# Attention scores of two heads in one four-bank PSUM tile, subtractions moved from POOL to DVE, more bias units ahead, and one account that shares work between DVE and ACT

## The chip, the cores and the metric

The kernel runs on one core of a Trainium2 chip. A core has five engines with a queue each: TensorE (PE, with PEld for the loading of its weights), VectorE (DVE), ScalarE (ACT), GpSimd (POOL) and SyncE (SP), which here issues the DMAs. Each engine takes its instructions in the order of its queue. The metric is the time of one execution on the device in microseconds (us); lower is better. All tensors are fp32 in DRAM.

## The reference

Attention with a learned relative bias (B = 2 batches, H = 8 heads, S = 576 positions, D = 64), then two gated feed-forward layers over 1152 tokens of 512 features with 1536 hidden features:

```python
scores = scale * (q @ k.T)                                   # per batch and head
x = log1p(abs(i - j)) / log1p(max(i, 1))                     # per pair of positions
bias = relu(x[..., None] @ w1 + b1) @ w2                     # 32 hidden features, 8 heads
attn = softmax(scores + bias); y = attn @ v                  # 2, 8, 576, 64
x = y.transpose(0, 2, 1, 3).reshape(1152, 512)
x = ((x @ w_a) * (x @ w_b)) @ w_out                          # first layer
x = (silu(x @ w_gate) * (x @ w_val)) @ w_out                 # second layer
```

## The kernel before, in words

**Products.** A matrix product in fp32 is made of three products of a rounded high part and a remainder: high by high, high by low, low by high. So q has the parts `qa` and `qb`, k has `ka` and `kb`, the attention's output `xh` and `xl`, the feed-forward weights `wh` and `wl`. A high part is a copy that rounds (a cast), a low part the source minus the high part (a subtraction).

**Bias units.** The bias of 16 rows for all eight heads is a unit; there are 36 (`Bias.make`, L119). A unit has four instructions `hidden` (L109 on DVE or L111 on ACT, tiles `hd`), four to eight matmuls (L133) into a one-bank PSUM tile `tp`, two to four instructions `scaled` (L115 on DVE or L117 on ACT) into `bt`, and one DMA that writes `bt` to `bias_d` in DRAM (L146). Whether DVE or ACT takes a `hidden` or a `scaled` is decided by `Bias.take` with an account of these instructions alone. Twelve units are emitted first (L303), then two in each of the first twelve steps (L309).

**Steps of the attention.** There are 20 steps, each for a pair of heads `p`, a group `g` of query tiles and one tile `t` of 128 rows (L307). Heads `2p` and `2p+1` lie on partitions 0 to 63 and 64 to 127 of q and k. A step loads its bias rows from `bias_d` (L325; for t = 4, the last 64 rows of both batches, into two padded tiles `pad`, L329), then calls `scores` (L231), once for each batch, or once for t = 4. A call of t < 4 has twelve matmuls (L238) of 288 columns: two halves of the columns, three products, two heads `j`; the two heads use different halves of the rows of the array. There are 32 such calls, and four of t = 4 with 24 matmuls of 320 columns. The results lie in two PSUM tiles `ps` of two banks, one for each head, from a pool of two (L216, L233). For each head one DVE instruction (L241) adds the bias, writes `es` to SBUF and finds the row maximum `nm`; ACT makes the exponential (L245). Then PE transposes `es` in chunks of 128 columns into `tp` (L263), and `keep` (L250) copies each three chunks to `ee`, on ACT (L253) ten times of sixteen, else on DVE (L255).

**The end of a pair and group** (`finish`, L266): row sums `rs` (L272 to L275, DVE), `rw` (L277, ACT), its transposes (L282), `rc` (L287, ACT), the products with v into `pu` (L291), `t` (L293, DVE), then the high part `xh` on ACT (L300) and the low part `xl` on POOL (L301). The q and k of the next pair are loaded by SP at the first step of a pair and split by `Heads.split`: cast on DVE (L157), subtraction on POOL (L158).

**The feed-forward stage** (`moe`, L372) starts after the attention. It has 2592 matmuls (L389) of 384 columns; DVE and ACT decode its weights (L201 to L207), and POOL subtracts (L208).

**What sets the order.** The program text is not the order of the queues. A scheduler simulates the engines, and puts each instruction into its engine's queue at the time at which it expects it to be ready; `issue_after` holds an instruction back behind another. Buffers are handed on as tiles come free.

Of the kernel before, what the change touches and what calls it, by code (L numbers as in the profile page):

```python
# [50 lines left out]
def attention_moe_moe(ctx: ExitStack, tc: tile.TileContext, qd, kd, vd, cst, lm, wm1, wm2, out):  # L51
# [10 lines left out]
    with (  # L62
        tc.tile_pool(name="prep", bufs=2) as prep,
        tc.tile_pool(name="a4", bufs=3) as a4,
    ):
        heads = Heads(tc, prep, qd, kd, vd)
        bias = ExitStack()
        bias.enter_context(tc.tile_pool(name="bc", bufs=1, side="right"))
        units = Bias(tc, bias, cst, lm, bias_d, heads)
        ends = attention(ctx, tc, a4, heads, bias, units, bias_d, xh, xl, weights, ident)  # L70
    moe(tc, xpool, xh, xl, weights, out, ends)


class Bias:
# [7 lines left out]
    def __init__(self, tc, stack, cst, lm, bias_d, heads):  # L82
        nc = self.nc = tc.nc
        self.tc, self.bias_d = tc, bias_d
# [15 lines left out]
        self.spent = {"dve": 0.0, "act": 0.0}  # L100

    def take(self, dve, act):
        eng = "dve" if self.spent["dve"] + dve <= self.spent["act"] + act else "act"
        self.spent[eng] += dve if eng == "dve" else act
        return eng == "dve"

    def hidden(self, dst, n, m):
        if self.take(DFIX + n * DMASK, AFIX + n * AELEM):
            self.nc.vector.tensor_scalar(dst, self.LW[:, :n], self.bp[:, m : m + 1], 0.0, op0=ALU.add, op1=ALU.max)  # L109
# [3 lines left out]
    def scaled(self, dst, src, n, u):  # L113
        if self.take(DFIX + n * DCOPY, AFIX + n * AELEM):
# [34 lines left out]
class Heads:  # L149


    def __init__(self, tc, pool, qd, kd, vd):
        self.nc, self.pool, self.d, self.got = tc.nc, pool, (qd, kd, vd), {}
# [57 lines left out]
def attention(ctx, tc, a4, heads, bias, units, bias_d, xh, xl, weights, ident):  # L211
    nc = tc.nc
    with (
        tc.tile_pool(name="ac", bufs=1, reuse_waits="tile") as cpool,
        tc.tile_pool(name="a2", bufs=2, reuse_waits="tile") as a2,
        tc.tile_pool(name="ps2", bufs=2, reuse_waits="tile", space=PSUM) as ps2,  # L216
# [14 lines left out]
        def scores(p, i, ops, n, es, bt):  # L231

            ps = [ps2.tile([P, 2, 512], F32, tag="big", name="ps") for j in range(2)]  # L233
            for hf in range(2):
                for m, (lt, rt) in enumerate(ops):
                    for j in range(2):
                        r = slice(64 * j, 64 * j + 64)
                        nc.tensor.matmul(ps[j][:, hf, :n], lt[r], rt[r, n * hf : n * hf + n], start=m == 0, stop=m == len(ops) - 1)  # L238
            for j in range(2):
                nm = a4.tile([P, 1], F32, tag="nm", name="nm")  # L240
                nc.vector.tensor_tensor_reduce(  # L241
                    out=es[j].rearrange("p (a j) -> p a j", a=2), in0=ps[j][:, :, :n], in1=bt[j].rearrange("p (a j) -> p a j", a=2),
                    op0=ALU.add, op1=ALU.min, scale=-0.125, scalar=3.0e38, accum_out=nm,
                )
                nc.scalar.activation(es[j], es[j], AF.Exp, bias=nm, scale=-1.0, accum_out=sums[:, 2 * p + j, i : i + 1])  # L245

        turn = [0]
# [18 lines left out]
        def finish(p, g, ee):  # L266
# [12 lines left out]
            for b in range(B):  # L279
# [7 lines left out]
                nc.scalar.copy(rc[:, :n], rb[:, :n])  # L287
# [5 lines left out]
                nc.vector.tensor_tensor(t1[:, :n], pu[:, :n], rc[:, :n], op=ALU.mult)  # L293
                s0 = place(b, g)
# [14 lines left out]
        made = (2, 2, 2, 2, 2, 2, 2, 2, 2, 2, 2, 2)  # L309
        ee = {}  # L310
        for idx, (p, g, t) in enumerate(steps):
            if idx < len(made):
# [206 lines left out]
```

## Time and profile before

| | us |
|---|---|
| median of three runs | 733.45 (731.39 to 737.64) |
| the profiled execution | 736.44 |
| its span from the first to the last instruction | 734.7 |
| PE busy in the span | 684.2 (93%) |
| DVE busy | 473.6 (64%) |
| ACT busy | 326.3 (44%) |
| POOL busy | 162.4 (22%) |

The profile is one execution; its times are in microseconds from the start of the span. Busy time of an engine counts overlapping instructions once. PEclk is the clock granted to TensorE as a share of full speed. In a timeline row, the bracket at the end is the idle time of the engine just before the instruction and what ended it. A row of the grouped view gives the count, the busy time, the mean nanoseconds of one, and the idle time ahead of the group with the releasers. The attention's score matmuls run from the first steps until about 250 us; the feed-forward stage follows.

### The profile page before, as it was taken

The numbers are of one execution on the slowest core, as the hardware profiler recorded it, in microseconds if no ns is written. First come the engines' busy times: TensorE is split into PE (matmuls) and PEld (weight loads), VectorE is DVE, ScalarE is ACT, GpSimd is POOL, SyncE is SP. The second block draws the span as 40 slices with busy tenths as digits, with TensorE's granted clock in tenths as the row PEclk, the third lists the DMA queues.
The fourth block names the chain that finished last, engine by engine and source line by source line (L and its number), as shares of the span: only waits on it lengthen the run. The fifth ranks groups of instructions, "written<-read, shape, count | busy, mean of one in ns | idle before, by whom it ended". The sixth has DMA issues, their size and how long they took to land. (4 is left out here: it accounts for less than half of the span.)

```text
span 734.7 us, 10847 instructions
## 1 busy us (share of the span) xinstructions
PE 684.2 (93%) x4112; PEld 597.1 (81%) x4112; DVE 473.6 (64%) x877; ACT 326.3 (44%) x688; POOL 162.4 (22%) x131
## 2 busy tenths in 40 slices
PE   5669699999999989999899999999989999999997
PEld 2236465656667769988899999999989999999997
DVE  7674676965677379999936993269951896232222
ACT  4636555767557456444413342245432552121110
POOL 3020051212332033332302332144410430020000
PEclk9985789999989999999999999999989999999999
DMA  3774345525566024443411440024330241000111
GB/s 108 206 237 153 113 140 178 155 66 187 164 226 181 7 87 144 144 139 118 145 58 33 137 146 29 1 72 130 118 112 1 89 153 45 1 1 1 44 43 44
DMA packets 26516, 76.35 MB, mean 104 GB/s; under 512 B 2656, under 2 KB 4320, under 8 KB 26464
## 3 DMA queue, kind: packets, MB, share of 16 engines
q1 hardware_dynamic: 26464, 75.66, 32.5%
q8 instruction: 32, 0.52, 0.3%
q14 instruction: 20, 0.16, 0.1%
HBM read 62.40 MB, written 13.25 MB: 103 GB/s over the span
## 5 line engine op out<-in xcount | busy, mean ns | idle before, releaser
L208 POOL TENSOR_TENSOR wl<-m,wh 128x512 fp32r<-128x512 f32 x72 | 99.9, 1390 | 253.8 <-ACT wh L207 223.3
L410 DVE TENSOR_TENSOR g<-p,g 128x384 f32<-128x384 f32 x72 | 39.8, 553 | 128.2 <-PE p L389 128.2
L389 PE MATMUL po<-gh,wh 128*128 128x384 f32 x288 | 98.5, 344 | 10.1 <-DVE acc L440 7.3
L389 PE MATMUL p<-xh,wh 128*128 128x384 f32 x288 | 97.2, 339 | 2.2 <-ACT g L409 2.2
L389 PE MATMUL po<-gh,wl 128*128 128x384 f32 x288 | 97.5, 339 | 0.0
L389 PE MATMUL po<-gl,wh 128*128 128x384 f32 x288 | 97.5, 339 | 0.0
L389 PE MATMUL p<-xl,wh 128*128 128x384 f32 x288 | 97.2, 338 | 0.0
L389 PE MATMUL p<-xh,wl 128*128 128x384 f32 x288 | 97.1, 337 | 0.0
L389 PE MATMUL p<-yh,wh 128*128 128x384 f32 x288 | 96.9, 337 | 0.0
L389 PE MATMUL p<-yh,wl 128*128 128x384 f32 x288 | 96.9, 337 | 0.0
L389 PE MATMUL p<-yl,wh 128*128 128x384 f32 x288 | 96.9, 336 | 0.0
L205 DVE SCALAR_TENSOR_TENSOR m<-raw,m 128x512 uint32<-128x512 uint32 x72 | 81.4, 1130 | 1.5
L412 ACT CAST gh<-g 128x384 fp32r<-128x384 f32 x72 | 36.9, 513 | 96.0 <-DVE g L410 96.0
L201 ACT ACTIVATE m<-raw 128x512 f32<-128x512 f32 x72 | 48.8, 679 | 61.1 <-POOL wl L208 60.1
L409 ACT ACTIVATE g<-p 128x384 f32<-128x384 f32 x72 | 34.9, 486 | 85.0 <-PE p L389 84.6
L245 ACT ACTIVATE es<-es,nm 128x576 f32<-128x576 f32 (+1 forms) x72 | 56.2, 782 | 27.3 <-DVE nm L241 26.4
L389 PEld LDWEIGHTS po<-gh,wh 128*128 128x128 f32 x288 | 54.7, 190 | 14.2 <-DVE acc L440 6.0
L207 ACT CAST wh<-m 128x512 fp32r<-128x512 f32 x72 | 44.2, 620 | 46.0 <-DVE m L206 42.5
L241 DVE CUSTOM_DVE_ANT_0 es<-ps,bt 128x576 f32<-128x576 f32 x64 | 46.9, 752 | 22.5 <-DMA bt<-bias_d 10.3
L263 PE MATMUL tp<-ident,es 128*128 128x128 f32 x328 | 55.0, 304 | 6.2 <-DVE bt L115 5.1
L238 PE MATMUL ps<-ka,qa 64*128 64x288 f32 (+1 forms) x160 | 52.1, 376 | 9.0 <-DVE nm L241 9.0
L206 DVE SCALAR_TENSOR_TENSOR m<-raw,m 128x512 uint32<-128x512 uint32 x72 | 58.8, 817 | 1.0
(64 smaller groups left out, 1278.2 us busy)
## 6 DMA issues: line engine op xcount, KB each, us to landing
raw<-in_wm SPq DMA_DIRECT2D x72, 512.0 KB
bias_d<-bt SPq DMA_DIRECT2D x36, 295.5 KB
bt<-bias_d SPq DMA_DIRECT2D x32, 288.0 KB
vv<-in_vd SPq DMA_DIRECT2D x8, 640.0 KB
kr<-in_kd SPq DMA_DIRECT2D x8, 576.0 KB
pad<-bias_d SPq DMA_DIRECT2D x16, 144.0 KB
out_t<-acc SPq DMA_DIRECT2D x12, 192.0 KB
raw<-in_qd SPq DMA_DIRECT2D x4, 352.0 KB
```

Source lines behind the costliest of these rows:

```text
L201: nc.scalar.activation(m, hi.bitcast(F32), AF.Abs)
L205: nc.vector.scalar_tensor_tensor(t, lo, 29, t, op0=ALU.logical_shift_right, op1=ALU.bitwise_or)
L206: nc.vector.scalar_tensor_tensor(t, hi, 0xC0000000, t, op0=ALU.bitwise_and, op1=ALU.bitwise_or)
L207: nc.scalar.copy(wh[:, i], m)
L208: nc.gpsimd.tensor_tensor(wl[:, i], m, wh[:, i].bitcast(F32), op=ALU.subtract)
L238: nc.tensor.matmul(ps[j][:, hf, :n], lt[r], rt[r, n * hf : n * hf + n], start=m == 0, stop=m == len(ops) - 1)
L241: nc.vector.tensor_tensor_reduce(out=es[j].rearrange("p (a j) -> p a j", a=2), in0=ps[j][:, :, :n], in1=bt[j].rearrange("p (a j) -> p a j" ...
L245: nc.scalar.activation(es[j], es[j], AF.Exp, bias=nm, scale=-1.0, accum_out=sums[:, 2 * p + j, i : i + 1])
L263: nc.tensor.transpose(tp[:, n], es[:, P * kc : P * kc + P], ident)
L389: nc.tensor.matmul(ps, lt, rt, start=first and n == 0, stop=last and n == len(parts) - 1)
L410: nc.vector.tensor_tensor(g, pp[1], g, op=ALU.mult)
L412: nc.scalar.copy(gh, g)
```

## The change

- `scores` writes to one PSUM tile of four banks for both heads, from a pool of one. The twelve matmuls are written in the same order.
- The low parts of q, k and of the attention's output are made on DVE instead of POOL. The low parts of the feed-forward weights, and of the output of the first layer, stay on POOL.
- The casts of q and k, `keep`, and the copy `rc` may be on DVE or ACT: one account `Share` of the work of both engines decides this, with `hidden` and `scaled`. It also counts, without choosing, the maxima and exponentials, the subtractions, `t` and `xh`. Its prices are new.
- `MADE` makes four units in each of the first two steps and two in each of the next eight.
- The calls of t = 4 are held behind the last DVE `hidden` of the twelfth unit (`lag`).

```diff
+MADE = (4, 4, 2, 2, 2, 2, 2, 2, 2, 2)
 HDS, BTS = 8, 4
-DFIX, DMASK, DCOPY = 160.0, 0.52, 1.04
-AFIX, AELEM = 280.0, 0.86
-
-SHARE = 10
+DFIX, DFAST, DSLOW = 70.0, 0.52, 1.04
+AFIX, AELEM = 190.0, 0.86
...
+class Share:
+    def __init__(self):
+        self.spent = [0.0, 0.0]
+
+    def dve(self, n, slope=DSLOW):
+        self.spent[0] += DFIX + n * slope
+
+    def act(self, n, more=0.0):
+        self.spent[1] += AFIX + n * AELEM + more
+
+    def on_dve(self, n, slope=DSLOW):
+        d, a = DFIX + n * slope, AFIX + n * AELEM
+        first = self.spent[0] + d <= self.spent[1] + a
+        self.spent[0 if first else 1] += d if first else a
+        return first
...
     def hidden(self, dst, n, m):
-        if self.take(DFIX + n * DMASK, AFIX + n * AELEM):
+        if self.share.on_dve(n, DFAST):
...
     def scaled(self, dst, src, n, u):
-        if self.take(DFIX + n * DCOPY, AFIX + n * AELEM):
+        if self.share.on_dve(n):
...
-        self.nc.vector.tensor_copy(hi[:, : n[0]], raw[:, : n[0]])
-        self.nc.gpsimd.tensor_tensor(lo[:, : n[0]], raw[:, : n[0]], hi[:, : n[0]].bitcast(F32), op=ALU.subtract)
+        w = n[0]
+        if self.share.on_dve(w, DFAST):
+            self.nc.vector.tensor_copy(hi[:, :w], raw[:, :w])
+        else:
+            self.nc.scalar.copy(hi[:, :w], raw[:, :w])
+        self.share.dve(w)
+        self.nc.vector.tensor_tensor(lo[:, :w], raw[:, :w], hi[:, :w].bitcast(F32), op=ALU.subtract)
...
-        tc.tile_pool(name="ps2", bufs=2, reuse_waits="tile", space=PSUM) as ps2,
+        tc.tile_pool(name="ps2", bufs=1, reuse_waits="tile", space=PSUM) as ps2,
...
-            ps = [ps2.tile([P, 2, 512], F32, tag="big", name="ps") for j in range(2)]
+            ps = ps2.tile([P, 2, 2, 512], F32, tag="big", name="ps")
...
-                        nc.tensor.matmul(ps[j][:, hf, :n], lt[r], rt[r, n * hf : n * hf + n], start=m == 0, stop=m == len(ops) - 1)
+                        nc.tensor.matmul(ps[:, j, hf, :n], lt[r], rt[r, n * hf : n * hf + n], start=m == 0, stop=m == len(ops) - 1)
...
+                share.dve(2 * n, 1.3)
+                share.act(2 * n, 190.0)
...
         def keep(dst, src):
-            turn[0] += 1
-            if turn[0] * SHARE % 16 < SHARE:
+            if share.on_dve(dst.free_size() if hasattr(dst, "free_size") else 384):
+                ends[1] = nc.vector.tensor_copy(dst, src)
+            else:
                 ends[0] = nc.scalar.copy(dst, src)
-            else:
-                ends[1] = nc.vector.tensor_copy(dst, src)
...
-                nc.scalar.copy(rc[:, :n], rb[:, :n])
+                if share.on_dve(n):
+                    nc.vector.tensor_copy(rc[:, :n], rb[:, :n])
+                else:
+                    nc.scalar.copy(rc[:, :n], rb[:, :n])
...
-                        nc.gpsimd.tensor_tensor(xl[c][:, p, a - CH * c : e - CH * c], src, dh.bitcast(F32), op=ALU.subtract)
+                        nc.vector.tensor_tensor(xl[c][:, p, a - CH * c : e - CH * c], src, dh.bitcast(F32), op=ALU.subtract)
...
+        lag = units.last
...
-                scores(p, 8, ops, 320, es, bt)
+                with tc.issue_after(lag.ins):
+                    scores(p, 8, ops, 320, es, bt)
```

What follows shows three places of the queues. A row names the line, the operation, the tiles it writes and reads (with the number of the buffer's tile) and its shape; `x2` stands for two in a row that read alike. L238 of before is L256 now, L263 is L281, L291 is L312, L241 is L259.

PE at the first call of a step (pair 0, tile 1) before: `ps_865` is the PSUM tile of the first head, `ps_866` that of the second.

```order
L238 MATMUL ps_865<-ka_109,qa_105 128x288
L238 MATMUL ps_865<-kb_110,qa_105 128x288
L238 MATMUL ps_865<-ka_109,qb_106 128x288
L238 MATMUL ps_865<-ka_109,qa_105 128x288
L238 MATMUL ps_865<-kb_110,qa_105 128x288
L238 MATMUL ps_865<-ka_109,qb_106 128x288
L263 MATMUL tp_795<-ident_65,es_753 128x128 x3
L238 MATMUL ps_866<-ka_109,qa_105 128x288
L238 MATMUL ps_866<-kb_110,qa_105 128x288
L238 MATMUL ps_866<-ka_109,qb_106 128x288
```

The same call now:

```order
L281 MATMUL tp_857<-ident_65,es_817 128x128 x3
L256 MATMUL ps_927<-ka_109,qa_105 128x288 x2
L256 MATMUL ps_927<-kb_110,qa_105 128x288 x2
L256 MATMUL ps_927<-ka_109,qb_106 128x288 x2
L256 MATMUL ps_927<-ka_109,qa_105 128x288 x2
L256 MATMUL ps_927<-kb_110,qa_105 128x288 x2
L256 MATMUL ps_927<-ka_109,qb_106 128x288 x2
L281 MATMUL tp_862<-ident_65,es_817 128x128 x3
```

Before, six matmuls of one head stand together and six of the other later; now the matmuls of the two heads stand in pairs, each pair reading both halves of the array's rows, as all calls do in the new queue.

PE at the seam of two steps late in the attention, as it is now: `ps_2002` is the second call of one step, `ps_2119` the first call of the next, and both are the same four banks.

```order
L281 MATMUL tp_2021<-ident_65,es_1981 128x128 x3
L256 MATMUL ps_2002<-ka_1631,qa_1627 128x288 x2
L256 MATMUL ps_2002<-kb_1632,qa_1627 128x288 x2
L256 MATMUL ps_2002<-ka_1631,qb_1628 128x288 x2
L256 MATMUL ps_2002<-ka_1631,qa_1627 128x288 x2
L256 MATMUL ps_2002<-kb_1632,qa_1627 128x288 x2
L256 MATMUL ps_2002<-ka_1631,qb_1628 128x288 x2
L281 MATMUL tp_2026<-ident_65,es_1981 128x128
L312 MATMUL pu_2061<-ee_1888,vv_1893 64x256
L256 MATMUL ps_2119<-ka_1903,qa_1899 128x288 x2
```

Between the two calls one transpose and one product are left, and both calls write to the same four banks. Before, `ps_2143` of the next step stood behind `ps_2026` at this place: the one took the two-bank tile of the first head, the other that of the second.

DVE at the first maximum, before: the two rows L241 are the maximum and the reading of its result.

```order
L109 TENSOR_SCALAR hd_321<-LW_92,bp_98 128x512
L115 TENSOR_SCALAR bt_283<-tp_282,cs_91 128x272
L109 TENSOR_SCALAR hd_323<-LW_92,bp_98 128x512
L115 TENSOR_SCALAR bt_306<-tp_304,cs_91 128x264
L241 ISA es4_440,nm_468<-ps_442,pad0_129 128x640
L241 ISA nm_468 128x1
```

The same place now:

```order
L122 TENSOR_SCALAR hd_342<-LW_92,bp_98 128x496
L122 TENSOR_SCALAR hd_353<-LW_92,bp_98 128x480
L122 TENSOR_SCALAR hd_357<-LW_92,bp_98 128x480
L122 TENSOR_SCALAR hd_359<-LW_92,bp_98 128x480
L122 TENSOR_SCALAR hd_370<-LW_92,bp_98 128x464
L128 TENSOR_SCALAR bt_328<-tp_327,cs_91 128x79
L122 TENSOR_SCALAR hd_374<-LW_92,bp_98 128x464
L122 TENSOR_SCALAR hd_376<-LW_92,bp_98 128x464
L259 ISA es4_474,nm_501<-ps_476,pad0_129 128x640
L259 ISA nm_501 128x1
L259 ISA es4_475,nm_504<-ps_476,pad1_130 128x640
```

Before, the first maximum stood behind hidden features of 512 columns, which are the ninth unit's, and ahead of those of the tenth to twelfth unit (496, 480 and 464 columns). Now all that DVE has of the twelve units' hidden features stands ahead of it.

## Rows read from the trace of the kernel before

**Rows 1.** Windows: length, busy PE, PEld, DVE, ACT, POOL, then PEclk, DMA share, GB/s.

```profile
0.00:60.00 60.00, 37.20 (x273) 17.99 (x273) 42.79 (x92) 31.57 (x63) 10.12 (x11) 0.87 0.60 183
60.00:90.00 30.00, 23.92 (x134) 16.35 (x134) 16.59 (x45) 16.99 (x40) 0.00 (x0) 0.67 0.39 126
90.00:250.00 160.00, 155.40 (x1059) 103.36 (x1058) 110.22 (x253) 102.43 (x254) 41.02 (x36) 0.95 0.50 151
300.00:540.00 240.00, 230.09 (x1299) 225.94 (x1297) 183.66 (x287) 96.02 (x175) 74.69 (x56) 0.99 0.30 97
```

**Rows 2.** The chain of waits that ended last, by engine, from the page.

```profile
PE 26%; DVE 5%; issue 1%; ACT 0%; DVEq 0%
```

**Rows 3.** Timeline (start, us) of score matmuls: pairs, one head alone, twelve.

```profile
17.20 0.32 PE L238 MATMUL ps<-kb,qa 64*128 64x320 f32 x2
17.34 0.32 PE L238 MATMUL ps<-ka,qb 64*128 64x320 f32 x2
...
248.36 0.40 PE L238 MATMUL ps<-ka,qa 64*128 64x288 f32 x1
...
249.35 0.44 PE L263 MATMUL tp<-ident,es 128*128 128x128 f32 x2
...
231.81 0.40 PE L238 MATMUL ps<-ka,qa 64*128 64x288 f32 x1
...
233.17 0.66 PE L263 MATMUL tp<-ident,es 128*128 128x128 f32 x4
```

**Rows 4.** Window, score matmuls alone: length, PE, PEld, PEclk, DMA share, GB/s.

```profile
90.00:250.00 160.00, 59.53 (x372) 47.90 (x370) 0.95 0.50 151
```

**Rows 5.** Timeline: waits for the bias on DVE and ACT before 90 us.

```profile
29.58 0.82 DVE L241 CUSTOM_DVE_ANT_0 es<-ps,pad 128x640 f32<-128x640 f32 x1 [3.70 <-DMA pad<-bias_d]
...
46.70 0.63 ACT L117 ACTIVATE bt<-tp,cs 128x448 f32<-128x448 f32 x1 [4.74 <-DMA bias_d<-bt]
...
88.64 0.76 DVE L241 CUSTOM_DVE_ANT_0 es<-ps,bt 128x576 f32<-128x576 f32 x1 [3.06 <-DMA bt<-bias_d]
```

**Rows 6.** Timeline: DVE and POOL at two splits of q and k.

```profile
7.83 0.75 DVE L157 CAST ka<-kr 128x1152 fp32r<-128x1152 f32 x1
8.50 4.71 DVE L109 TENSOR_SCALAR hd<-LW,bp 128x560 f32<-128x560 f32 x2
...
13.33 0.50 DVE L109 TENSOR_SCALAR hd<-LW,bp 128x576 f32<-128x576 f32 x1
...
10.09 2.82 POOL L158 TENSOR_TENSOR kb<-kr,ka 128x1152 fp32r<-128x1152 f32 x1
...
42.27 3.43 DVE L109 TENSOR_SCALAR hd<-LW,bp 128x416 f32<-128x416 f32 x3
```

**Rows 7.** Source L272: durations in ns, min/median/max.

```profile
L272 DVE TENSOR_SCALAR rs<-sums x8: 158/173/2446, 96.3 to 251.2; 128x8 f32<-128x8 f32 x8
```

**Rows 8.** Grouped view by form, DVE: count, busy us, mean ns, idle before.

```profile
L157 DVE CAST ka<-kr 128x1152 fp32r<-128x1152 f32 x8 | 9.9, 1238 | 0.1
L293 DVE TENSOR_TENSOR t<-pu,rc 128x320 f32<-128x320 f32 x8 | 3.9, 487 | 13.9 <-PE pu L291 13.9
L293 DVE TENSOR_TENSOR t<-pu,rc 128x256 f32<-128x256 f32 x8 | 3.4, 423 | 7.8 <-PE pu L291 7.8
L255 DVE COPY ee<-tp 128x384 f32<-128x384 f32 x40 | 22.0, 550 | 14.3 <-PE tp L263 14.3
L241 DVE CUSTOM_DVE_ANT_0 es<-ps,bt 128x576 f32<-128x576 f32 x64 | 46.9, 752 | 22.5 <-DMA bt<-bias_d 10.3 <-PE ps L238 7.1 <-ACT es L245 2.4
```

**Rows 9.** Timeline and windows at a change of TensorE's clock.

```profile
215.41 0.44 PE L238 MATMUL ps<-kb,qa 64*128 64x288 f32 x1
215.65 0.44 PE L238 MATMUL ps<-ka,qb 64*128 64x288 f32 x1
...
210.00:215.00 5.00, 3.72 (x27) 2.85 (x27) 4.63 (x12) 4.66 (x12) 2.57 (x3) 1.00 0.78 300
215.00:222.00 7.00, 7.00 (x29) 5.31 (x29) 6.15 (x13) 4.17 (x11) 1.77 (x1) 0.51 0.30 73
```

More of the change, by code (lines that the diff above doesn't have):

```diff
@@ L65, in attention_moe_moe, with __init__ @@
     ):
-        heads = Heads(tc, prep, qd, kd, vd)
+        share = Share()
+        heads = Heads(tc, prep, qd, kd, vd, share)
         bias = ExitStack()
         bias.enter_context(tc.tile_pool(name="bc", bufs=1, side="right"))
-        units = Bias(tc, bias, cst, lm, bias_d, heads)
-        ends = attention(ctx, tc, a4, heads, bias, units, bias_d, xh, xl, weights, ident)
+        units = Bias(tc, bias, cst, lm, bias_d, heads, share)
+        ends = attention(ctx, tc, a4, heads, share, bias, units, bias_d, xh, xl, weights, ident)
     moe(tc, xpool, xh, xl, weights, out, ends)
+class Share:
[10 more added lines that the diff above has]
+        return first
 class Bias:
-    def __init__(self, tc, stack, cst, lm, bias_d, heads):
+    def __init__(self, tc, stack, cst, lm, bias_d, heads, share):
         nc = self.nc = tc.nc
-        self.tc, self.bias_d = tc, bias_d
+        self.tc, self.bias_d, self.share = tc, bias_d, share
         bc = self.bc = stack.enter_context(tc.tile_pool(name="bm", bufs=1, side="right"))
@@ L99, in __init__ @@
             heads.load(0, 0)
[L100 to L105, printed above, removed]
     def hidden(self, dst, n, m):
-        if self.take(DFIX + n * DMASK, AFIX + n * AELEM):
-            self.nc.vector.tensor_scalar(dst, self.LW[:, :n], self.bp[:, m : m + 1], 0.0, op0=ALU.add, op1=ALU.max)
+        if self.share.on_dve(n, DFAST):
+            self.last = self.nc.vector.tensor_scalar(dst, self.LW[:, :n], self.bp[:, m : m + 1], 0.0, op0=ALU.add, op1=ALU.max)
         else:
@@ L149, with __init__ @@
 class Heads:
-    def __init__(self, tc, pool, qd, kd, vd):
-        self.nc, self.pool, self.d, self.got = tc.nc, pool, (qd, kd, vd), {}
+    def __init__(self, tc, pool, qd, kd, vd, share):
+        self.nc, self.pool, self.d, self.got, self.share = tc.nc, pool, (qd, kd, vd), {}, share
     def split(self, raw, n, tags, bufs):
         hi, lo = (self.pool.tile([P, n[1]], F32R, tag=x, name=x, bufs=bufs) for x in tags)
-        self.nc.vector.tensor_copy(hi[:, : n[0]], raw[:, : n[0]])
-        self.nc.gpsimd.tensor_tensor(lo[:, : n[0]], raw[:, : n[0]], hi[:, : n[0]].bitcast(F32), op=ALU.subtract)
+        w = n[0]
[5 more added lines that the diff above has]
+        self.nc.vector.tensor_tensor(lo[:, :w], raw[:, :w], hi[:, :w].bitcast(F32), op=ALU.subtract)
         return hi, lo
@@ L208, in part, with attention @@
         nc.gpsimd.tensor_tensor(wl[:, i], m, wh[:, i].bitcast(F32), op=ALU.subtract)
-def attention(ctx, tc, a4, heads, bias, units, bias_d, xh, xl, weights, ident):
+def attention(ctx, tc, a4, heads, share, bias, units, bias_d, xh, xl, weights, ident):
     nc = tc.nc
@@ L241, in scores @@
                 nc.vector.tensor_tensor_reduce(
-                    out=es[j].rearrange("p (a j) -> p a j", a=2), in0=ps[j][:, :, :n], in1=bt[j].rearrange("p (a j) -> p a j", a=2),
+                    out=es[j].rearrange("p (a j) -> p a j", a=2), in0=ps[:, j, :, :n], in1=bt[j].rearrange("p (a j) -> p a j", a=2),
                     op0=ALU.add, op1=ALU.min, scale=-0.125, scalar=3.0e38, accum_out=nm,
                 )
+                share.dve(2 * n, 1.3)
+                share.act(2 * n, 190.0)
                 nc.scalar.activation(es[j], es[j], AF.Exp, bias=nm, scale=-1.0, accum_out=sums[:, 2 * p + j, i : i + 1])
-        turn = [0]
         ends = [None, None]
         def keep(dst, src):
-            turn[0] += 1
-            if turn[0] * SHARE % 16 < SHARE:
+            if share.on_dve(dst.free_size() if hasattr(dst, "free_size") else 384):
+                ends[1] = nc.vector.tensor_copy(dst, src)
+            else:
                 ends[0] = nc.scalar.copy(dst, src)
-            else:
-                ends[1] = nc.vector.tensor_copy(dst, src)
         def bank():
@@ L293, in finish @@
                 nc.vector.tensor_tensor(t1[:, :n], pu[:, :n], rc[:, :n], op=ALU.mult)
+                share.dve(n)
+                share.dve(n)
+                share.act(n)
                 s0 = place(b, g)
@@ L308, in attention @@
         steps += [(p, 0, t) for p in (2, 3) for t in TILES[0]] + [(p, 1, t) for p in range(4) for t in TILES[1]]
-        made = (2, 2, 2, 2, 2, 2, 2, 2, 2, 2, 2, 2)
         ee = {}
         for idx, (p, g, t) in enumerate(steps):
-            if idx < len(made):
-                for _ in range(made[idx]):
+            if idx < len(MADE):
+                for _ in range(MADE[idx]):
                     units.make(rest.pop(0), bank)
```

## The prediction

> **What bounds the kernel now.** I read the chain of waits first. It ends in PE's work (26% of the span) with short pieces of DVE [rows 2], and behind the attention PE is busy 230.09 of 240 us at a clock of 0.99 [rows 1]. The change touches nothing there, so the feed-forward stage keeps its length, and the question is when the attention ends. The windows split it in two. From 90 to 250 us PE is busy 155.40 of 160, DVE 110.22, ACT 102.43 [rows 1]: PE is the bound, and what PE no longer has to do is worth its time, as long as DVE lets it go on. From 0 to 90 us PE is busy 61 (37.20 and 23.92), DVE 59 (42.79 and 16.59) [rows 1]: no engine is full, and it is waits that set the length, among them waits for the bias through DRAM [rows 5] and DVE instructions that stretch beside POOL [rows 6].
>
> **Part 1, scores in pairs.** Two matmuls that use different halves of the array's rows run side by side when they stand together: the pairs of t = 4 start 0.145 us apart (17.20 to 17.34) [rows 3], so one matmul takes half of that. Before, most calls are cut into six of one head and six of the other. One such six takes 0.99 us (248.36 to 249.35), two 1.98; twelve that stood together took 1.36 (231.81 to 233.17) [rows 3]. All calls are pairs now. The best price of a call is that of six singles, 0.99, the worst the 1.36 just read; I take 1.13, nearer the best, since the pairs of t = 4 follow one another without a gap. From 90 to 250 us score matmuls keep PE busy 59.53 us [rows 4]. There lie 28 calls of t < 4 and two of t = 4 (12 pairs of 0.145 and a fill, 2.0). New: 28 x 1.13 + 2 x 2.0 = 35.6 us. PE's work falls by 59.5 - 35.6 = 24, from 155.4 to **131.5** (128 to 138 at the two ends).
>
> **Part 2, one tile instead of two.** Each call now waits until both maxima of the call before have read the four banks, and PE has only transposes, bias units and pu products in between. The maximum takes 0.752 us in the mean [rows 8], two in a row some 1.5. In most places the transposes of the step before fill that. At the seam of two steps, which the second place of PE's order shows, one transpose and one product are left, and even four transposes last only 0.66 [rows 3]; 1.5 - 0.66 = 0.84, and with the hand-over between the engines I take 1.0 us. The 16 steps after 90 us have 15 seams: **15 us** of stall, 0 if the scheduler's order covers them, 30 if DVE has a copy or a subtraction in front of the maxima. So 131.5 + 15 = 146.5 against 160: 13.5 less.
>
> **Part 3, DVE takes POOL's subtractions.** What goes: beside POOL's subtraction DVE instructions stretch. Two hidden instructions took 4.71 us while POOL worked on kb until 12.91, and one of 576 columns, the widest, took 0.50 right behind [rows 6]: 3.7 lost. The cast of k is 0.75 alone and 1.238 in the mean of eight: 8 x 0.49 = 3.9 lost [rows 6, 8]. The sums of L272 have a median of 0.173 and a maximum of 2.446 [rows 7]: at least 2.3 lost in the longest, at most 4 x 2.3 = 9 if the upper half of the eight are as long; I take 5. Three hidden instructions took 3.43 [rows 6], 1.9 over 3 x 0.50. The hidden instructions' 5.6 lie before 60 us, the other 8.9 I put behind 90. What comes: a subtraction with two sources is like L293, whose 64 columns more cost 0.064 us (0.487 against 0.423) [rows 8], 1.0 ns a column. So 1152 columns cost 1.32, 704 0.87, 512 0.68. The set of a pair is 2.2 or 2.0; two sets lie before 90 us (4.4), six after (2 x 2.2 + 4 x 2.0 = 12.4). The 20 pieces of xl (8 of 256, 8 of 128, 4 of 320) cost 0.42, 0.28 and 0.49: 7.6. From below: nothing, where DVE is idle anyway; from above, twice that, where the queue behind a subtraction waits on it, since DVE is in order and the maxima queue behind it and PE behind them.
>
> **Part 4, the account.** By the new queues DVE takes 63 of the 128 copies of `keep` instead of 48, some 13 more of them after 90 us at 0.55 [rows 8]: +7.2. Four `rc` of about 0.45 add 1.8, and ten of sixteen casts leave DVE, about -4 there. DVE after 90 us: 110.2 - 8.9 + 12.4 + 7.6 + 7.2 + 1.8 - 4 = **126 us** of 146.5, 86% against 69% before. It fits, with 20 us to spare, and so I leave the sum at PE's.
>
> **Part 5, the order before 90 us.** The first maximum waited 3.70 us for `pad`, ACT 4.74 for a slot of `bt`, the maximum at 88.64 waited 3.06 [rows 5]: 11.5 us of waits for the bias. Now all twelve units' hidden work of DVE stands ahead of the first maximum (third place shown), and eight units instead of four are made in the first two steps, with their DMAs ahead of the loads. These waits go, with 5.6 of stretched DVE work, against 4.4 of new subtractions: 12.7. The bias rows must be written before they are read, however, and DVE reaches its first maximum later; what is late next is the sum of hidden work on DVE and ACT. I count half, **-6.5**, with ends 0 and -16.
>
> **The sum.** -6.5 - 13.5 + 0 = -20. Beside the profiled execution's 736.44 us that is 716.4; the median of 733.45 is 3.0 below it, so **713 us**.
>
> A rule speaks against part 1. The Trainium skill's TensorEngine Tiling (Array Packing), section PSUM Bottleneck, says that running several row tiles at once speeds up TensorE but not the evacuation of PSUM, which may become the bottleneck. By it the 24 us of part 1 would be worth only what DVE leaves, and the case R2 below would hold.
>
> **Rivals.**
>
> R1, the full gain. The scheduler fills the seams, the early waits all go: 160 falls to 135 (-25) and the first 90 us by 16: 736.4 - 41 - 3 = 692; I put the case at 692 to 704. For it: DVE has room, and DVE's stretched work goes in full. Against: the seam leaves one transpose and one product between two calls that need the same banks.
>
> R2, the account does not balance. Its DVE price of a copy of 384 columns is 70 + 384 x 1.04 = 469 ns, measured 550 [rows 8]; of a hidden instruction of 560 columns 361, while 0.50 is measured at 576 [rows 6]. Each is too low, so DVE gets more than its share; its waits for PE and ACT do not vanish. Of 160 us DVE was idle 50 [rows 1]; with 126 us of work, idle time of 34 takes all of part 1. The gain then is that of the early part alone, or none: 726 to 741. For it: a DVE that is in order and stands between PE and PE at each call. Against: much of the idle time was waiting for PE, which is faster now.
>
> R3, the clock; this is the one that ends slower. PE works in bursts with an idle stretch at each seam. After 5 us in which PE was busy 3.72, the granted clock was 0.51 for 7 us [rows 9], which is the level of 1.2 GHz against 2.4, and matmuls there start 0.24 apart (215.41 to 215.65) [rows 9]; by the pairs' 0.145 for 320 columns [rows 3], 288 take 0.13 at the upper level. From 60 to 90 us the clock is 0.67 with PE busy 23.92 of 30 [rows 1]. If a share x of the 131.5 us of PE's work after 90 us falls to the lower level, it costs x times 0.85 times 131.5, which is 112 x, more. From 713 the time reaches 741 when x is 0.25; at 0.4 it is 713 + 45 = 758. Range 741 to 758. For it: 15 seams with an idle stretch of 1 us. Against: PE was kept at 0.95 through all of 90 to 250 [rows 1], and one stall of that length is not followed everywhere by a fall.
>
> The Trainium skill's TensorE: Matmul & The Clock Gate, section on psum-queue depth-cycling, describes just this: a kernel that cycles through PSUM banks leaves PE idle for moments between groups of matmuls, its clock goes up and down, and the throughput falls. No run here shows it for one four-bank tile; the 7 us at 0.51 agree in kind.
>
> **How the numbers follow.** The forecast case (704 to 726: part 2 between 8 and 26 us, the early part between 0 and -12) has 0.61, R1 0.12, R2 0.17, R3 0.10. A change of 1%, 7.3 us, is about what a measurement of this kernel can tell from none. Below 726.1 lie the forecast, R1 and an edge of R2: **0.74** faster. Within 1%: the rest of R2, **0.16**. Above 740.8: R3, **0.10**. The predicted time is the forecast's own, 713. The range that holds 8 in 10 reaches from **698** (the upper half of R1; 0.06 lies below) to **738** (four fifths of R2; its last part and R3, 0.13, lie above).
>
> **What would show it.** Part 1: the score matmuls' busy time behind the fifth step's first maximum falls from 59.5 to near 36 us, all of them in pairs, and a call lasts 1.0 to 1.2 us. Part 2: PE's idle time at the first score matmul of a step names the maximum's result `nm`, about 1 us each. Part 3: no DVE instruction of the attention over twice its usual duration, and POOL without work there but for the weights. Part 5: the waits of DVE for `pad` and of ACT for `bt` gone before 90 us. The last score matmul would end near 230 us instead of 250. I am wrong if PE's granted clock between 90 and 230 us falls below 0.85 (R3), if DVE is over 90% busy there and PE waits for `nm` more than 2 us a step (R2), or if the first maximum that uses `bt` comes later than before.

## The result and the profile after

The changed kernel takes 714.68 us (median of 4 runs, 714.12 to 716.56), the kernel before 734.67 (4 runs, 731.39 to 737.64): a ratio of **0.973**, 95% interval 0.969 to 0.978. Forecast were 713 us and a range of 698 to 738. The profiled execution takes 716.56 us, 19.9 below that of before. The sum came out; two of its three terms did not, and the experiments tell in part why. (Of the kernel with the old order of units, below, the profiled execution was disturbed, at a clock of 0.83, and is left out.)

Windows of the changed kernel, with the columns of [rows 1]; the second begins, near the one from 90 us in [rows 1], at the fifth step's first maximum, which stands now at 82.4 us instead of 88.64 [rows 5], and ends in the last maximum:

```profile
0.00:82.40 82.40, 53.71 (x409) 25.93 (x410) 55.29 (x149) 48.41 (x100) 0.74 (x7) 0.83 0.60 184
82.40:239.40 157.00, 134.92 (x1056) 84.67 (x1056) 115.43 (x295) 102.37 (x241) 3.85 (x3) 0.96 0.50 152
260.00:715.00 455.00, 442.82 (x2526) 439.02 (x2524) 291.13 (x465) 164.51 (x308) 108.07 (x79) 0.99 0.24 80
```

The score matmuls of that stretch alone (columns as in [rows 4]):

```profile
82.40:239.40 157.00, 35.75 (x372) 27.76 (x372) 0.96 0.50 152
```

Three pairs of one call, from the timeline of PE (as in [rows 3]):

```profile
197.50 0.40 PE L256 MATMUL ps<-ka,qa 64*128 64x288 f32 x2
197.74 0.29 PE L256 MATMUL ps<-kb,qa 64*128 64x288 f32 x2
197.87 0.29 PE L256 MATMUL ps<-ka,qb 64*128 64x288 f32 x2
```

PE's busy time in the late stretch falls by 21 us, that of the score matmuls alone by 24 (59.53 to 35.75), but the stretch is only 4 us shorter: PE sits idle 157.0 - 134.9 = 22 us of it, against 5 before. Where the 19.9 us of the two profiled executions lie, by five marks in each trace (differences are of the unrounded times):

| stretch | before | after | difference | forecast |
|---|---|---|---|---|
| start to the fifth step's first maximum | 88.6 | 82.4 | -6.2 | -6.5 |
| from there to the end of the last maximum | 161.6 | 157.7 | -3.9 | -13.5 |
| to the end of the last pu product | 15.3 | 15.0 | -0.2 | (in the line above) |
| feed-forward stage to the last matmul | 464.7 | 455.6 | -9.1 | 0 |
| to the end of the span | 4.5 | 4.0 | -0.5 | 0 |

What PE waited for, from the grouped view of PE between 82.4 and 239.4 us (idle before, then releasers):

```profile
L281 PE MATMUL tp<-ident,es 128*128 128x128 f32 x270 | 44.6, 297 | 12.0 <-ACT es L265 5.5 <-ACT ee L273 3.5 <-DVE ee L271 2.7
L256 PE MATMUL ps<-ka,qa 64*128 64x288 f32 (+1 forms) x124 | 23.3, 353 | 8.1 <-DVE nm L259 7.8
```

The maxima make 7.8 us of it; 12.0 us come before transposes, in the exponentials and copies. The longest single stall, in a timeline of ACT and PE:

```profile
161.25 0.62 ACT L174 CAST qa<-raw 128x512 fp32r<-128x512 f32 x1 [4.72 <-DMA raw<-in_qd]
162.75 1.15 ACT L174 CAST ka<-kr 128x1152 fp32r<-128x1152 f32 x1 [0.88 <-DMA kr<-in_kd]
163.81 0.77 ACT L265 ACTIVATE es<-es,nm 128x576 f32<-128x576 f32 x1
164.72 1.54 PE L281 MATMUL tp<-ident,es 128*128 128x128 f32 x6 [4.95 <-ACT es L265]
```

Two windows of it, with the columns of [rows 1]:

```profile
160.00:165.00 5.00, 0.28 (x2) 0.28 (x3) 1.76 (x2) 2.87 (x5) 0.00 (x0) 0.82 0.56 197
165.00:170.00 5.00, 5.00 (x27) 4.06 (x27) 3.50 (x11) 3.44 (x9) 0.00 (x0) 0.50 0.05 16
```

A cast that the account gave to ACT waits for its load of q; the exponentials stand behind it in ACT's queue, PE's transposes behind those, and for 5 us after the stall the granted clock is 0.50, the lower level.

At the seam to the feed-forward stage, before (timeline of POOL, ACT and PE):

```profile
263.45 1.37 POOL L301 TENSOR_TENSOR xl<-t,xh 128x128 fp32r<-128x128 f32 x2 [14.51 <-ACT xh L300]
264.78 2.96 POOL L208 TENSOR_TENSOR wl<-m,wh 128x512 fp32r<-128x512 f32 x2
267.77 0.67 ACT L201 ACTIVATE m<-raw 128x512 f32<-128x512 f32 x1 [0.56 <-POOL wl L208]
268.35 0.85 ACT L409 ACTIVATE g<-p 128x384 f32<-128x384 f32 x2
268.87 0.44 PE L389 MATMUL p<-xh,wh 128*128 128x384 f32 x1 [2.15 <-ACT g L409]
```

and after:

```profile
254.07 2.58 POOL L226 TENSOR_TENSOR wl<-m,wh 128x512 fp32r<-128x512 f32 x2 [35.57 <-ACT wh L225]
255.99 0.48 ACT L434 ACTIVATE g<-p 128x384 f32<-128x384 f32 x1
256.53 0.44 PE L414 MATMUL p<-xh,wh 128*128 128x384 f32 x1 [0.17 <-ACT g L434]
```

Before, `xl` on POOL stood ahead of the weights' subtraction, ACT waited for the buffer that this frees, and ACT's `g` behind it held PE for 2.15 us. Now it is 0.17.

### The profile page after: what moved, and what is told of

Its sections match the earlier page's. It is cut to its first block, busy times and chain, and to the rows that moved or that the text cites. A ratio compares the mean times of both kernels' runs of the same rounds, so it can differ in the third digit from the quotient of the medians.

```text
span 714.8 us, 10832 instructions
## 1 busy us (share of the span) xinstructions
PE 650.9 (91%) x4112; PEld 565.8 (79%) x4112; DVE 473.7 (66%) x934; ACT 325.5 (46%) x671; POOL 115.2 (16%) x91
## 5 line engine op out<-in xcount | busy, mean ns | idle before, releaser
L226 POOL TENSOR_TENSOR wl<-m,wh 128x512 fp32r<-128x512 f32 x72 | 101.5, 1413 | 482.6 <-ACT wh L225 453.3
L281 PE MATMUL tp<-ident,es 128*128 128x128 f32 x328 | 55.3, 300 | 25.4 <-DVE bt L128 9.5
L281 PEld LDWEIGHTS tp<-ident,es 128*128 128x128 f32 x328 | 37.7, 148 | 45.9 <-DVE bt L128 11.0
L146 PE MATMUL tp<-hd,cs 128*32 128x264 f32 (+17 forms) x352 | 43.9, 540 | 13.8 <-DVE hd L122 6.7
```

Source lines behind the costliest of these rows:

```text
L146: nc.tensor.matmul(ps[a][32 * cg : 32 * cg + 32, :w], self.W2, hd[cg][:, w * a : w * a + w], start=True, stop=True)
L226: nc.gpsimd.tensor_tensor(wl[:, i], m, wh[:, i].bitcast(F32), op=ALU.subtract)
L281: nc.tensor.transpose(tp[:, n], es[:, P * kc : P * kc + P], ident)
```

## The experiments

Theory A is the forecast's own account. Theory B: the pairs' saving is given back in stalls. Theory C: with one tile every delay of DVE lies between two calls, so POOL's stretching of DVE, priced at nothing after 90 us, is what decides. The others are named where they come. Ratios are to the kernel before, timed beside each kernel: its median was 734.67 us beside the changed kernel, 733.65 beside the first four kernels below, 731.15 beside those of the old order, the old sharing, the casts and POOL's loads, and 733.23 beside the rest; its single runs lie between 726 and 741. So a difference of 3 or 4 us from the changed kernel's 714.68 is not shown by the times alone.

**The scores in two tiles again** (all else as changed).

```diff
-        tc.tile_pool(name="ps2", bufs=1, reuse_waits="tile", space=PSUM) as ps2,
+        tc.tile_pool(name="ps2", bufs=2, reuse_waits="tile", space=PSUM) as ps2,
...
-            ps = ps2.tile([P, 2, 2, 512], F32, tag="big", name="ps")
+            ps = [ps2.tile([P, 2, 512], F32, tag="big", name="ps") for j in range(2)]
...
```

> The changed kernel with the scores again in two tiles of two banks; all else as changed. In the new queue all calls of t < 4 are cut into single matmuls of one head. Theory A (the forecast's terms hold: pairs save 24 us of PE, the seams give 15 back): 714.7 + 9 = 723 to 725. Theory B (the pairs' saving is given back nearly whole, since in the changed kernel PE sits idle 22 us between the maximum at 82 us and the end of the scores, against 5 before): 715 to 718. In both, PE's idle time of that stretch falls back below 8 us, and the score matmuls' busy time goes from 36 to near 60.

Measured: 722.62 us (720.89 to 723.23), ratio 0.985 (0.979 to 0.992), 7.9 above the changed kernel. The time is theory A's, not B's. The traces do not show the gain where A has it: between the same two maxima (window below) this kernel takes 157.9 us and the changed one 157.7. PE's idle time there is 3.4 us in this kernel and 22.1 in the changed one, its busy time 154.5 and 134.9, so in these two executions, 4.3 us apart as a whole, the pairs' saving is given back, as B has it.

```profile
84.36:242.25 157.89, 154.48 (x1071) 103.07 (x1072) 116.78 (x303) 104.32 (x247) 3.85 (x3) 0.98 0.51 151
```

**The four-bank tile alone**, in the kernel before.

```diff
-        tc.tile_pool(name="ps2", bufs=2, reuse_waits="tile", space=PSUM) as ps2,
+        tc.tile_pool(name="ps2", bufs=1, reuse_waits="tile", space=PSUM) as ps2,
...
-            ps = [ps2.tile([P, 2, 512], F32, tag="big", name="ps") for j in range(2)]
+            ps = ps2.tile([P, 2, 2, 512], F32, tag="big", name="ps")
...
```

> The kernel before with the four-bank tile alone; POOL, the account and the order of the units as before. Theory A: 734 - 9 = 724 to 727. Theory B: 730 to 735, the score matmuls' busy time behind 88 us near 36, and PE's idle time there over 17 us. If POOL's stretching of DVE now lies on the path from maximum to matmul, it is slower than before: 736 to 745.

Measured: 735.2 us (10 runs, 729.81 to 737.18), ratio 1.003 (0.998 to 1.007). Theory A falls: alone, the tile gives nothing, though the score matmuls go in pairs. The time lies between theory B's case and the slower one, and B's sign is there: PE is idle 26 of the 169.9 us between the two maxima, with 40.0 us of score matmuls.

**The subtractions of q, k and x on POOL again** (the account leaves them out).

```diff
-        self.share.dve(w)
-        self.nc.vector.tensor_tensor(lo[:, :w], raw[:, :w], hi[:, :w].bitcast(F32), op=ALU.subtract)
+        self.nc.gpsimd.tensor_tensor(lo[:, :w], raw[:, :w], hi[:, :w].bitcast(F32), op=ALU.subtract)
...
-                        nc.vector.tensor_tensor(xl[c]...)
+                        nc.gpsimd.tensor_tensor(xl[c]...)
```

> The changed kernel with the subtractions of q, k and x on POOL again; the account leaves them out. Theory A (after 90 us PE is the bound, so the stretched DVE work costs nothing there; early 5.6 of stretch against 4.4 of subtractions): 714 to 718. Theory C (with one tile each DVE delay lies between two calls, so the 9 to 14 us of stretched DVE work come back on the path): 722 to 729.

Measured: **735.78 us** (10 runs, 734.4 to 736.49), ratio 1.002 (0.999 to 1.005): all of the gain is gone. C is right in kind, and too small. Of the 18.4 us between the two profiled executions, 11.6 lie between the two maxima and 7.0 in the feed-forward stage. How the first part comes about, from this kernel's timeline:

```profile
134.34 0.85 DVE L172 CAST ka<-kr 128x1152 fp32r<-128x1152 f32 x1
135.11 3.26 DVE L122 TENSOR_SCALAR hd<-LW,bp 128x512 f32<-128x512 f32 x2
135.32 2.76 POOL L175 TENSOR_TENSOR kb<-kr,ka 128x1152 fp32r<-128x1152 f32 x1 [0.75 <-POOL qb L175]
138.29 0.55 DVE L270 COPY ee<-tp 128x384 f32<-128x384 f32 x1
138.89 0.55 PE L280 MATMUL tp<-ident,es 128*128 128x128 f32 x3 [1.92 <-DVE ee L270]
...
210.72 2.82 POOL L175 TENSOR_TENSOR kb<-kr,ka 128x1152 fp32r<-128x1152 f32 x1
210.97 3.12 DVE L223 SCALAR_TENSOR_TENSOR m<-raw,m 128x512 uint32<-128x512 uint32 x1
214.61 0.90 PE L280 MATMUL tp<-ident,es 128*128 128x128 f32 x3 [1.76 <-DVE ee L270]
```

DVE is held up beside the subtraction of 1152 columns, a copy stands behind, and PE waits for the copy. So it goes with DVE at seven of the eight subtractions of that size. Beside the eighth DVE had maxima and a copy from PSUM, and they were not stretched:

```profile
168.34 2.64 POOL L175 TENSOR_TENSOR kb<-kr,ka 128x1152 fp32r<-128x1152 f32 x1 [1.12 <-DVE rs L289]
169.06 0.76 DVE L258 CUSTOM_DVE_ANT_0 es<-ps,bt 128x576 f32<-128x576 f32 x1 [0.52 <-PE ps L255]
169.74 0.55 DVE L270 COPY ee<-tp 128x384 f32<-128x384 f32 x1
```

The window of 82.4 to 240 us, and ten microseconds in it:

```profile
82.40:240.00 157.60, 130.92 (x971) 81.39 (x970) 111.51 (x252) 88.26 (x212) 39.67 (x33) 0.89 0.49 149
...
210.00:220.00 10.00, 6.21 (x34) 4.19 (x36) 10.00 (x18) 5.74 (x13) 5.10 (x4) 0.60 0.40 122
```

PE is idle 27 us in 157.6, 5 more than in the changed kernel, and the clock is 0.89 in the mean, against 0.96 there, and 0.60 in the ten microseconds in which DVE was held up. That is what rival R3 expected to see; the next kernel shows that idle time alone does not account for the clock.

**The subtractions alone on DVE**, in the kernel before.

```diff
-        self.nc.gpsimd.tensor_tensor(lo[:, : n[0]], ...)
+        self.nc.vector.tensor_tensor(lo[:, : n[0]], ...)
...
-                        nc.gpsimd.tensor_tensor(xl[c]...)
+                        nc.vector.tensor_tensor(xl[c]...)
```

> The kernel before with the subtractions of q, k and x on DVE, all else as before. Theory A: 731 to 734, since DVE is not the bound. Theory C in its weaker form (two tiles hide a DVE delay better): 727 to 731. If the 20 us of subtractions delay the maxima behind them in DVE's queue: 736 to 742.

Measured: 727.75 us (10 runs, 725.97 to 729.22), ratio 0.993 (0.989 to 0.997): 6 us. The time is that of theory C's weaker form, but the place is another. The last maximum ends at 250.0 us here and at 250.2 before, so the attention is no shorter; the feed-forward stage is, by 7.6 us. The fifth step's first maximum stands at 79.9 us here, without any change of the order, and the stretch behind it is 8.4 us longer than before (170.0). The clock of that stretch is 0.90, with PE idle for no more than 5.8 us:

```profile
79.94:249.95 170.01, 164.24 (x1061) 108.61 (x1062) 114.95 (x290) 104.61 (x255) 3.83 (x3) 0.90 0.48 146
```

**The subtraction of x alone on POOL** in the changed kernel, and, in another run, **those of q and k alone**; the account leaves out what is moved.

```diff
-                        nc.vector.tensor_tensor(xl[c]...)
+                        nc.gpsimd.tensor_tensor(xl[c]...)
```
```diff
-        self.nc.vector.tensor_tensor(lo[:, :w], ...)
+        self.nc.gpsimd.tensor_tensor(lo[:, :w], ...)
```

> The changed kernel with only the subtraction of x (xl) on POOL again. Theory E (in the kernel before, xl stands in POOL's queue ahead of the weights' subtractions at the seam to the feed-forward stage, and holds up ACT and then PE, 2.15 us at 268.9 us, with a slower clock behind it): the idle time of PE in the feed-forward stage rises from 8 to 11 or 12 us, and the time to 718 to 723. If that stage's length only varies from run to run: 714 to 716 and 8 us of idle time.

> The changed kernel with only the subtractions of q and k on POOL again. Theory C (stretched DVE work lies on the path between two calls of the one tile): the larger part of the 21 us of both comes back here, 726 to 732, with idle time of PE in the feed-forward stage still at 8 us. If the x subtraction was the dear one: 715 to 719.

Measured: x on POOL 718.35 us (716.65 to 720.99), 3.7 above the changed kernel; q and k on POOL 728.3 (10 runs, 726.98 to 731.03), 13.6 above. Both expectations hold. PE's idle time in the feed-forward stage is 10.9 us with x on POOL, 8.1 with q and k there; the stall is this row of the first of the two:

```profile
258.49 0.44 PE L413 MATMUL p<-xh,wh 128*128 128x384 f32 x1 [1.77 <-ACT g L433]
```

In the four traces with x on POOL this idle time is 12.2 (before), 10.9 (the tile alone), 12.5 and 10.9; of the nine read here with x on DVE, 8.0 or 8.1 in each.

**The old order of units**: two units in each of twelve steps, no hold of the t = 4 calls.

```diff
-MADE = (4, 4, 2, 2, 2, 2, 2, 2, 2, 2)
+MADE = (2,) * 12
...
-                with tc.issue_after(lag.ins):
-                    scores(p, 8, ops, 320, es, bt)
+                scores(p, 8, ops, 320, es, bt)
```

> The changed kernel with two units in each of the first twelve steps again, and the t = 4 calls not held back. Theory A (the early term of the forecast, -6.5, comes from this order): 719 to 722. Theory D (the early gain comes from the stretched DVE work that is gone, and the order only moves the waits for the bias, since in the changed kernel a maximum still waits 5.40 us for pad at 33 us and ACT 18 us in six waits for a slot of bt): 713 to 717.

Measured: 716.0, 716.04 and 717.43 us, ratio 0.980 (0.973 to 0.988). By the times the order is worth 1 to 3 us, as theory D has it; by the ratios (0.980 against 0.973) it is 5. Less than the 6.5 of theory A is likely, not shown.

**The old rule of sharing**: hidden and scaled by an account of their own, ten of sixteen copies and `rc` on ACT, casts on DVE.

```diff
-            if share.on_dve(dst.free_size() if hasattr(dst, "free_size") else 384):
+            turn[0] += 1
+            if turn[0] * SHARE % 16 >= SHARE:
...
-DFIX, DFAST, DSLOW = 70.0, 0.52, 1.04
-AFIX, AELEM = 190.0, 0.86
+DFIX, DFAST, DSLOW = 160.0, 0.52, 1.04
+AFIX, AELEM = 280.0, 0.86
```

> The changed kernel with the old rule of sharing: hidden and scaled by the old account of their own, ten of sixteen copies on ACT, casts on DVE, rc on ACT. Subtractions stay on DVE, one tile, the new order of units. If the account is worth something by its own: 718 to 724, with ACT and DVE of the late stretch further apart than now (102 and 115 us). If it is worth nothing, or its low prices for DVE hurt (rival R2): 708 to 716.

Measured: **711.25 us** (709.4 to 711.95), ratio 0.973 (0.966 to 0.979), 3.4 less than the changed kernel, at the same ratio to the kernel before. No gain of the account is shown; a small loss is likely, since the last maximum ends at 233.2 us here and at 240.1 in the changed kernel, with the feed-forward stage alike (455.8 and 455.6). By the grouped view DVE has 40 copies of 384 columns instead of 53, and its busy time between the two maxima is 111.25 of 153.7 us instead of 115.43 of 157.0:

```profile
L271 DVE COPY ee<-tp 128x384 f32<-128x384 f32 x40 | 22.0, 550 | 5.5 <-PE tp L281 5.5
```

The window between the two maxima:

```profile
79.30:233.00 153.70, 133.54 (x1056) 84.02 (x1056) 111.25 (x284) 102.90 (x254) 3.80 (x3) 0.96 0.52 155
```

The wait for the load of q is here too, now in DVE's queue, as its timeline and PE's show:

```profile
157.51 0.43 DVE L172 CAST qa<-raw 128x512 fp32r<-128x512 f32 x1 [5.03 <-DMA raw<-in_qd]
159.44 0.61 PE L254 MATMUL ps<-ka,qa 64*128 64x288 f32 x2 [5.46 <-DVE nm L257]
```

**The casts on DVE**, counted by the new account.

```diff
-        if self.share.on_dve(w, DFAST):
-            self.nc.vector.tensor_copy(hi[:, :w], raw[:, :w])
-        else:
-            self.nc.scalar.copy(hi[:, :w], raw[:, :w])
+        self.share.dve(w, DFAST)
+        self.nc.vector.tensor_copy(hi[:, :w], raw[:, :w])
```

> The changed kernel with all casts of q and k on DVE, still counted in the account. In the changed kernel a cast of q at the head of ACT's queue waits 4.72 us for its load at 161 us, the exponentials stand behind it, and PE waits 4.95 us for them and runs slower for some 5 us after. If the place of the cast is the cause: 708 to 711. If the wait only moves to DVE's queue, where the maxima stand behind it: 713 to 717.

Measured: 718.23 us (717.47 to 719.08), 3.5 above the changed kernel; neither expectation holds. PE waits 5.31 us for a maximum at 159 us: the wait moves to DVE's queue. That it costs more there is not shown: the last maximum ends at 239.9 us, and at 240.1 in the changed kernel.

**The loads of q and k on POOL's queue.**

```diff
-        nc.sync.dma_start(raw[:, :n], self.d[0][p][:, g * QW[0] : g * QW[0] + n])
+        nc.gpsimd.dma_start(raw[:, :n], self.d[0][p][:, g * QW[0] : g * QW[0] + n])
...
-        nc.sync.dma_start(kr, self.d[1][p])
+        nc.gpsimd.dma_start(kr, self.d[1][p])
```

> The changed kernel with the loads of q and k issued by POOL's queue, which is empty in the attention, instead of SP's, where they stand behind loads of bias rows that wait for a free buffer. If the late load is the cause of the stall at 161 us, the stall and the slower clock behind it go, 5 to 8 us: 706 to 710. If the casts are late for another reason (the buffers qa and ka come free late): 713 to 716. If loads that start earlier push the bias writes and reads back on the shared DMA engines: 716 to 722.

Measured: 711.32 us (708.45 to 712.01), 3.4 less than the changed kernel. The load of q leaves at 132.51 us, with no bias rows ahead of it; in the changed kernel it left at 153.24:

```profile
132.51 0.62 POOL L182 DMA_DIRECT2D raw<-in_qd  x1 [30.55 <-DVE qb L176]
```

The window in which PE stood still in the changed kernel is at work:

```profile
160.00:165.00 5.00, 4.63 (x37) 2.82 (x37) 3.97 (x12) 4.70 (x11) 0.46 (x1) 1.00 0.83 239
```

The stall was expected to give 5 to 8. The time fell by 3.4, and by the ratio (0.972, 0.964 to 0.980) it is not clear of the changed kernel's; in the trace the last maximum ends 6.8 us earlier. A new wait is there: ACT waits 5.20 us for the first weight tile at 191 us, and PE 3.23 for ACT's copy at 193.

**The old sharing and POOL's loads together, and with the first weight tiles loaded earlier.**

```diff
-                if (p, g, t) == (2, 1, 2):
+                if (p, g, t) == (0, 1, 2):
```

The first of the two runs is without this line.

> The old rule of sharing (as in the run without the account, 711.3) and the loads of q and k by POOL's queue (711.3 with the account). There a cast waited 5.03 us on DVE for its load and PE 5.46 us behind it. If the two gains are separate ones: 706 to 709. If they are the same stall, taken away twice: 710 to 712.

> The run before this one, with the first three weight tiles of the feed-forward stage loaded four steps earlier (at the third group's first step, not the seventh's). With the old rule of sharing ACT waits 3.27 and 0.54 us for these loads at 198 us, with exponentials and copies behind it. If that wait lies on PE's path: 3 to 5 us less than best1, 702 to 705. If the decoding of the weights only moves to a place where DVE is as busy: no change.

Measured: 713.39 us (712.11 to 714.7) and 711.22 (709.56 to 711.87). The two gains of 3.4 do not add up: together they come to 1.3, and with the earlier weights to 3.5. In the second kernel ACT waits 4.46 us for the weights at 159 us, and PE 8.26 for a maximum:

```profile
159.46 0.66 ACT L217 ACTIVATE m<-raw 128x512 f32<-128x512 f32 x1 [4.46 <-DMA raw<-in_wm]
163.87 0.61 PE L254 MATMUL ps<-ka,qa 64*128 64x288 f32 x2 [8.26 <-DVE nm L257]
```

The wait for a load moves along the queue. The three kernels at 711 (ratios 0.972, 0.973 and 0.971) lie below the changed kernel in time; none of them stands clear of the others, nor by its ratio of the changed kernel's 0.973.

Two marks of each trace, in us:

| kernel | last maximum ends | feed-forward stage |
|---|---|---|
| before; the tile alone; the subtractions alone | 250.2; 251.2; 250.0 | 464.7; 458.0; 457.1 |
| changed, with subtractions on POOL: all; q and k; x | 250.0; 248.0; 240.4 | 462.6; 457.4; 459.7 |
| changed; with two tiles; with the casts on DVE | 240.1; 242.3; 239.9 | 455.6; 456.9; 457.4 |
| old sharing; POOL's loads; both; both and earlier weights | 233.2; 233.3; 235.4; 234.8 | 455.8; 457.1; 454.3; 454.2 |

## Why the prediction was right, and which of its steps failed

**Part 1, scores in pairs: right.** Forecast -24 us of PE's work, measured 59.53 to 35.75. A pair starts 0.13 us behind the other. (The sum counted 28 calls of t < 4; the 372 matmuls of [rows 4] are 27 such calls and two of t = 4, which is 1.1 us less.)

**Part 2, the stall of one tile: right in size, wrong in place.** Forecast 15 us at the seams; PE's idle time rose by 17 (5 to 22). Only 7.8 of the 22 are waits for a maximum, in rows of 0.5 to 1.6 us; 12.0 stand before transposes, led by the wait for exponentials behind a late cast. With the subtractions on DVE the tile is worth 7.9 us in time, close to the 9 of parts 1 and 2; the two traces have the late stretch equally long, so where these 7.9 come from stays open.

**Part 3, the subtractions: the step that failed.** The forecast took the stretched DVE work at 5.6 against 4.4 before 90 us and at nothing after, since PE was the bound there. Put back on POOL they cost 21.1 us. PE is the bound only as long as two tiles let it run ahead of DVE: its idle time in the late stretch is 3 to 6 us in the three traces with two tiles, on whichever engine the subtractions are. With one tile DVE stands in the chain between two calls, and what holds DVE up holds PE up: 18 to 25 us with q and k on DVE, 26 to 28 with them on POOL. The clock of the stretch is lower there too (0.89 to 0.92, against 0.93 to 0.97 with one tile and q and k on DVE), but the subtractions alone, with two tiles, had 0.90, so what lowers it is not settled. Of the 21.1, q and k alone cost 13.6 and x alone 3.7; the remaining 3.8 are within what such differences can tell.

The parts do not add: the subtractions alone give 6 us, the tile alone nothing (1.5 slower, within its interval), the whole change 20. No run has these two alone together. The runs that have both and lack the new order or the new sharing are at 716 and 711 us, and the tile, the order and the sharing without the subtractions at 735.8; with two tiles all the rest is at 722.6. So beside one tile hardly anything is gained without the subtractions. What the order and the sharing give with two tiles and POOL's subtractions no run shows.

**Part 4, the account: nothing in the sum, and no gain measured.** DVE's busy time was 115, not 126, of 157 us, so it was not overloaded as a whole. With the rest of the change the old rule is 3.4 us faster in time and level by the ratio. R2's mechanism, too low prices for DVE, is not shown by that: the account also moved the casts and `rc`, and the prices alone were not tried.

**Part 5, before 90 us: the right number, and its cause is open.** -6.2 against -6.5. I gave it to the order of the units. But the mark of 88.6 us is the latest of all traces. It stands at 79.9 with the subtractions alone and at 81.3 with the tile alone, both in the old order, and at 80.7 in the changed kernel with the subtractions on POOL. Each part seems to bring the mark alone, and in the first two of these kernels the last maximum ends no more than 0.2 us earlier for it, so a part of the 6 us may belong to the one execution of the kernel before. The waits for the bias did not go: `pad` still holds a maximum for 5.40 us at 33 us, and ACT waits 18 us in six waits for a slot of `bt`; the wait of the maximum at 88.64 us is gone.

**"The feed-forward stage keeps its length": wrong.** The change does touch its start, by the subtraction of x. The stage fell by 9.1 us between the two traces. Some 4 are PE's idle time (12.2 to 8.1), and the x subtraction is its cause: with x alone on POOL the stage is 4.1 us longer again, in a time that is 3.7 longer. The other 5 are matmuls that ran slower: the granted clock is at its lower level for 13.6 us of the stage before (from 269.6, 365.2 and 539.3 us on) and for 3.4 after (from 521.6 us on). The kernel before was slower in this stage than the other traces (454 to 463 us), so part of that belongs to the one execution that was profiled.

So -6.5, -13.5 and 0 came out as -6.2, -4 and -9. The late stretch gave 9 less than forecast, and the stage priced at nothing gave 9. The total was right by the luck of that balance, not by its terms.

**The rivals.** R1's full gain did not come: the early waits stayed. R3 was not far: with one tile and POOL's subtractions the clock of the late stretch was 0.89, and the time 735.8. The Trainium skill's TensorE: Matmul & The Clock Gate, section on psum-queue depth-cycling, has a clock that goes up and down with short idle times between groups of matmuls; that kernel agrees, and the changed one in single places (0.50 from 165 to 170 us), but the subtractions alone had a clock of 0.90 with 5.8 us of idle time. The rule of the Trainium skill's TensorEngine Tiling (Array Packing), section PSUM Bottleneck, held in part: of PE's 22 us of idle time, 7.8 are waits for the maxima and 6.2 for the copies, which empty PSUM, and the tile's 7.9 us are a third of the 24 saved on PE.

## What to carry to other kernels

Before one buffer takes the place of two, list everything in the queue of the engine that empties it: a delay that two buffers hide can reach the other engine behind one. Price two parts of a change together where one removes a cover and the other a delay; here they are worth nothing and 6 us alone, and taking the second away beside the first costs 21. Set a mark's gain beside the end of the stage: here a mark moved by 9 us, and the attention ended no earlier. And an instruction that waits for a load belongs behind the short work that others wait for: moved between ACT and DVE it took its stall with it, and earlier loads only moved the stall to the next one.

## What the runs showed of the hardware that was not expected

While POOL subtracted 1152 columns, some DVE instructions beside it ended only with it or behind it: hidden instructions of 512 columns (two in 3.26 us) and a weight instruction (3.12 us, where the median of the 72 such ones in this trace is 0.69). A maximum (0.76 us) and a copy from PSUM (0.55) beside another such subtraction kept their usual durations. The Trainium skill's GPSIMD Engine Reference, section Specifications, says that POOL shares its SBUF interfaces with DVE, with contention where DVE runs in a 2-port mode or has two SBUF inputs; the weight instruction, which reads two tiles, agrees, as do the maximum and the copy, which read no more than one tile of SBUF; in which mode the hidden ones run no run shows. A cast of 1152 columns took 1.15 us on ACT and 0.75 on DVE, an order that the account's prices (1181 and 669 ns) have right; a copy of 384 columns from PSUM took 550 ns on DVE, where they say 469.
